# First product of the seven-product blocks in matmuls of 128 tokens instead of 256

## The chip, the cores and the metric

The kernel runs on one NeuronCore of a Trainium2 chip. The metric is the device time of one execution in microseconds. The kernel before took 926.25 us (median of three runs, 922.67 to 926.61).

## The reference, cut to what matters

The program computes a windowed attention with some global tokens, and passes its output through a two-layer network with an ELU between the layers:

```python
x = np.ascontiguousarray(attn_out.transpose(0, 2, 1, 3)).reshape(B * S, H * D)   # 8 * 544 tokens, 512 wide
h = x @ w_in                                                                     # 512 -> 2048
g = np.where(h > 0.0, h, alpha * (np.exp(np.minimum(h, 0.0)) - 1.0))
return (g @ w_out).astype(np.float32)                                            # 2048 -> 512
```

The attention has 8 batches of 8 heads, 512 local tokens and 32 global tokens of width 64; a local token sees the local tokens within 32 places of it and the global ones.

## The kernel before, in words

**Precision.** The network's operands are split into two f16 parts, a high and a low one (xh and xl for the tokens, win[0] and win[1] for the first weights, and so on). A product is made of three f16 products: high by high, low by high, high by low. All add up in one f32 bank of PSUM. In the profile, winh and winl are the two parts of the first weights.

**Blocks.** The tokens are cut into 17 blocks of 256 (NBL = 16 and one of global tokens). For each block the function ffn1 makes the first product, for one pair p of 128-column groups of the 2048 hidden columns at a time (eight pairs, NP = 8). Its result h has hidden columns on the 128 partitions, and j (which group of the pair) and 256 tokens along a row of one PSUM bank. The weights are the stationary operand: each matmul loads 128x128 of them (LDWEIGHTS, in the profile on the engine named PEld) and streams the tokens. For each j, four row groups c of the 512 inputs times three part products make 12 matmuls, so a pair has 24 (line 316). ScalarE then makes relu, copy and exp of h (lines 326 to 328).

**Two kinds of second product.** Early blocks, while the weights are still being converted, use the plain second product (ffn2, line 440, 512 columns a matmul); their h lies in a tile named h. From about 291 us on, blocks use a product of 2 x 2 quarters with seven multiplications instead of eight (ffn2_seven, line 475, table SEVEN). For these the job carries a list `seven`, and h is taken from the pool ps_a, as a tile named pa. The quarters are sums and differences of 128-token halves of the two groups j, made by VectorE (lines 335 to 351), scaled to a high f16 part by ScalarE (line 354) and a low one by VectorE (line 338). A pair's second product has 21 matmuls of 256 columns. The last pair of the last block has a function of its own, ffn1_last (line 394).

**Order of the work.** ffn_stream is a generator. A pair of a block is one call of ffn1, then the ffn2_seven of an older pair; each yields several times, ffn1 in the middle of each j, between the two j and at the end. The main loop at the end of attn_ffn takes a step of the attention and then as many steps of ffn_stream as the table PACE (and a few holds and alignments, such as `at[0]`) ask for. So the attention's score matmuls (line 734), value matmuls (795) and transposes (789, 721) stand between pieces of the network's matmuls, in the order in which the generators yield. Much of the rest is put off by a number of steps with defer.

**PSUM flags.** A matmul with start set begins a sum; with start unset it adds to the columns, or, where these have not been written since the bank was begun, writes them.

Of the kernel before, what the change touches and what calls it, by code (L numbers as in the profile page):

```python
# [22 lines left out]
P = 128  # L23
# [4 lines left out]
BLK = 256  # L28
NC = DM // P
# [31 lines left out]
def attn_ffn(ctx: ExitStack, tc: tile.TileContext, qT, qgT, kT, vT, w_in, w_out, mask, out):  # L61
    nc = tc.nc
# [22 lines left out]
    def defer(n, fn):  # L85
        if n == 0:
            return fn()
        later.setdefault(now[0] + n, []).append(fn)
# [11 lines left out]
    at = [None]  # L100
# [15 lines left out]
    def turn(name, tiles):  # L116
        turns[name] += 1
        return tiles[turns[name] % len(tiles)]
# [23 lines left out]
    win = [wts.tile([P, NC, DF], F16, name=f"win{k}") for k in "hl"]  # L142
# [155 lines left out]
    def ffn_stream():  # L298
# [3 lines left out]
        def ffn1(job, p):  # L302
            group, blk, xh, xl, sc, seven = job
            if (blk, p) == (order[-1], NP - 1):
                yield from ffn1_last(job, p)
                return
            if seven is not None:
                h = ps_a.tile([P, 512], F32, name="pa").rearrange("p (j t) -> p j t", j=2)
            else:
                h = ps_h.tile([P, 2, BLK], F32, name="h")  # L310
            for j in range(2):
                f = slice((2 * p + j) * P, (2 * p + j + 1) * P)
                k = 0
                for c in range(NC):
                    for wt, xt in ((win[0], xh), (win[0], xl), (win[1], xh)):
                        nc.tensor.matmul(h[:, j, :], wt[:, c, f], xt[:, c, :], start=k == 0, stop=k == 11)  # L316
                        k += 1
                        if k == 6:
                            at[0] = None
                            yield  # L320
                if j == 0:
                    yield
            g = ffn.tile([P, 2 * BLK], F32, name="g", bufs=2)
            hs = turn("hs", hss)
            hf = h.rearrange("p j t -> p (j t)")
            nc.scalar.activation(g, hf, AF.Relu, scale=sc[:, p:p + 1])  # L326
            nc.scalar.activation(hs, hf, AF.Copy, scale=sc[:, 2 * NP + 1 + p:2 * NP + 2 + p])
            nc.scalar.activation(g, g, AF.Exp, scale=-1.0)  # L328
            sg = sc[:, NP + p:NP + p + 1]
            shape = [P, 2 * BLK] if seven is None else [P, 7, P]  # L330
            gh = ffn.tile(shape, F16, name="gh", bufs=3)
            gl = ffn.tile(shape, F16, name="gl", bufs=3)

            def elu(out, *ins):
                nc.vector.scalar_tensor_tensor(out=out, in0=ins[0], scalar=-1.0, in1=ins[1], op0=ALU.add, op1=ALU.max)  # L335

            def low(dst, src, hi):
                nc.vector.scalar_tensor_tensor(out=dst, in0=src, scalar=sg, in1=hi, op0=ALU.mult, op1=ALU.subtract)  # L338

            def plain():  # L340
                elu(g, g, hs)
                nc.scalar.activation(gh, g, AF.Copy, scale=sg)
                defer(1, lambda: low(gl, g, gh))

            def parts():

                gx, q = quarters()
                elu(q, *(a.rearrange("p (a x) -> p a x", x=P) for a in (g, hs)))
                nc.vector.tensor_add(gx[:, 2:4, :], q[:, 0:2], q[:, 2:4])  # L349
                nc.vector.tensor_sub(gx[:, 5:7, :], q[:, 0:4:2], q[:, 1:4:2])  # L350
                nc.vector.tensor_add(gx[:, 0, :], q[:, 1], q[:, 2])  # L351

                def high():
                    nc.scalar.activation(gh, gx, AF.Copy, scale=sg)  # L354

                def lows():
                    low(gl, gx, gh)
                    seven.append(p)

                defer(2, high)  # L360
                defer(4, lows)

            defer(*(2, plain) if seven is None else (4, parts))
            pend.append((job, p, gh, gl))
            yield

        def quarters():


            a = ffn.tile([P, 10, P], F32, name="gx", bufs=1)  # L370
            return a[:, 2:9, :], a[:, 0:10:3, :]
# [248 lines left out]
        while left <= NBL:  # L620
            load()
            job = job or choose()
            if job is None:
                yield True
                continue
            cur, job = job, None
            group, blk = cur[:2]
            lo, hi = GROUPS[group]
            for p in range(lo, hi):
                load()  # L630
                yield from ffn1(cur, p)
                if len(pend) > LAG2:
                    yield from ffn2()
                    if twice[0]:
                        twice[0] = False
                        if pend[0][1] in (pend[0][0][5] or ()):
                            yield from ffn2()
                if p == hi - 1:
                    job = choose()
            if group in "ef":  # L640
                del xs[blk]
                left += 1
# [324 lines left out]
    f = ffn_stream()  # L967
# [105 lines left out]
```

## Time and profile before

| | |
|---|---|
| median of three runs | 926.25 us |
| the profiled execution | 926.27 us |
| its span, first to last instruction | 924.5 us |
| TensorE (PE) busy | 95% of the span |
| weight loads (PEld) busy | 78% |
| VectorE (DVE) busy | 76% |
| ScalarE (ACT) busy | 69% |
| GpSimd (POOL) busy | 19% |
| mean granted TensorE clock | 0.984 |

A row of the groups has line, engine, operation, tile written and tiles read, size, number of instructions, then busy time and mean length of one, then idle time of the engine ahead of them and what ended it. PE is the matmul itself, PEld the load of its weights, which overlaps other matmuls. A matmul's record lasts longer than the time until the next one starts. The table of stretches has one row for a stretch of time, with each engine's busy time and number of instructions. A row of the chain of waits has start, length, and the engine, tile and line of a piece of the work that ended last. A row of the waits has who waited for whom, us in total, times, and the longest.

### The profile page before, as it was taken

Reading aid. Unit: us, or ns where it says so; the run is one execution under the profiler, and the core shown is the slowest. Engines: PE = TensorE matmul, PEld = TensorE weight load, DVE = VectorE, ACT = ScalarE, POOL = GpSimd, SP = SyncE. Lnnn points to the kernel's source line nnn. Section 1 sums busy time; section 2 is a strip of 40 time slices with the busy share of each in tenths; the row PEclk is TensorE's granted clock in tenths of the full one; section 3 lists DMA queues with packets and bytes.
Section 4 is the critical chain, followed back from the end, with each engine's and each line's share of the span. In section 5 each row is a group of like instructions: output and inputs, shape, how many; then the busy total and the mean of one; then the engine's idle time right before and its main releaser. Section 6 shows DMA issues by size and latency. Waiting matters only on the chain.

```text
span 924.5 us, 26174 instructions
## 1 busy us (share of the span) xinstructions
PE 881.6 (95%) x10737; PEld 722.0 (78%) x10737; DVE 703.0 (76%) x1949; ACT 637.4 (69%) x1458; POOL 175.8 (19%) x237
## 2 busy tenths in 40 slices
PE   6889988899999999999999999999999999999997
PEld 3557655566666888888888888888888888888886
DVE  4987998898679878686777768676878677766566
ACT  5779987876666667666757667676767676656564
POOL 3343542424121201101101011110110011200000
PEclk8899999999999999999999999999999999999999
DMA  7977965635443144013321234104301111000000
GB/s 260 351 261 250 315 203 179 198 148 186 159 160 130 42 165 151 5 68 120 134 71 49 69 127 151 49 26 170 135 20 69 47 48 47 1 24 24 1 24 23
DMA packets 41775, 107.78 MB, mean 117 GB/s; under 512 B 6200, under 2 KB 6840, under 8 KB 41656
## 3 DMA queue, kind: packets, MB, share of 16 engines
q1 hardware_dynamic: 41368, 105.86, 33.1%
q8 instruction: 84, 1.38, 0.6%
q14 instruction: 35, 0.29, 0.1%
q10 hardware_dynamic: 288, 0.26, 0.1%
HBM read 88.80 MB, written 17.30 MB: 115 GB/s over the span
## 4 chain that ended last, share of the span: by engine, by line
PE 44%; DVE 28%; ACT 20%; issue 4%; DMA 3%; POOL 1%; SPq 0%; DVEq 0%; ACTq 0%; POOLq 0%
PE pa L316 17%; PE acc L475 8%; PE h L475 6%; ACT p L752 5%; ACT gh L354 4%; DVE gl L338 4%; DVE gx L335 3%; PE h L316 3%; PE acc L440 3%; ACT g L326 2%; PE pa L795 2%; ACT g L328 2%; DVE gx L349 2%; DVE cu L191 2%; PE pa L789 1%
## 5 line engine op out<-in xcount | busy, mean ns | idle before, releaser
L316 PEld LDWEIGHTS <-winh 128*128 128x128 f16 x2160 | 209.5, 98 | 32.9 <-issue 2.9
L316 PE MATMUL pa<-xh,winh 128*128 128x256 f16 x824 | 224.8, 273 | 0.3 <-DVE xglob L865 0.2
L316 PE MATMUL pa<-xl,winh 128*128 128x256 f16 x824 | 224.6, 273 | 0.0
L316 PE MATMUL pa<-xh,winl 128*128 128x256 f16 x824 | 224.6, 273 | 0.0
L354 ACT ACTIVATE gh<-gx,xs 128x896 f16<-128x896 f32 x103 | 107.5, 1044 | 134.4 <-DVE gx L351 134.4
L338 DVE SCALAR_TENSOR_TENSOR gl<-gx,xs,gh 128x896 f16<-128x896 f32 x103 | 122.7, 1191 | 73.2 <-ACT gh L354 73.2
L475 PEld LDWEIGHTS <-gh 128*128 128x128 f16 x1456 | 140.2, 98 | 22.7 <-issue 7.2
L758 POOL TENSOR_TENSOR p<-p,sm 128x512 f32<-128x512 f32 x64 | 72.4, 1134 | 343.9 <-DVE sm L757 310.9
L752 ACT ACTIVATE p<-p,m 128x128 f32<-128x128 f32 x256 | 99.3, 390 | 27.9 <-DVE m L746 27.8
L316 PEld LDWEIGHTS <-winl 128*128 128x128 f16 x1080 | 106.0, 98 | 13.1 <-issue 0.4
L475 PE MATMUL acc<-wouth,gh 128*128 128x256 f16 x312 | 85.2, 273 | 0.1
L328 ACT ACTIVATE g<-g 128x512 f32<-128x512 f32 x135 | 85.1, 631 | 0.0
L475 PE MATMUL acc<-wouth,gl 128*128 128x256 f16 x312 | 85.1, 273 | 0.0
L475 PE MATMUL acc<-woutl,gh 128*128 128x256 f16 x312 | 85.0, 273 | 0.0
L475 PEld LDWEIGHTS <-gl 128*128 128x128 f16 x728 | 71.2, 98 | 9.4 <-DVE gl L338 1.2
L326 ACT ACTIVATE g<-pa,xs 128x512 f32<-128x512 f32 x103 | 70.3, 682 | 8.8 <-PE pa L316 8.0
L475 PE MATMUL h<-raw,gh 128*128 128x256 f16 x416 | 74.3, 273 | 0.0
L316 PE MATMUL h<-xh,winh 128*128 128x256 f16 x256 | 70.6, 276 | 0.0
L316 PE MATMUL h<-xh,winl 128*128 128x256 f16 x256 | 70.6, 276 | 0.0
L316 PE MATMUL h<-xl,winh 128*128 128x256 f16 x256 | 70.5, 275 | 0.0
L795 PEld LDWEIGHTS pa<-pt,v 128*64 128x64 f32 x1728 | 52.9, 138 | 7.9 <-issue 5.9
L335 DVE SCALAR_TENSOR_TENSOR gx<-g,p 128x512 f32<-128x512 f32 x52 | 35.9, 691 | 27.4 <-ACT g L328 26.1
(228 smaller groups left out, 1891.4 us busy)
## 6 DMA issues: line engine op xcount, KB each, us to landing
v<-vT SPq DMA_DIRECT2D x64, 512.0 KB, 4.7
k<-kT SPq DMA_DIRECT2D x32, 640.0 KB, 5.3
q<-qT SPq DMA_DIRECT2D x32, 256.0 KB, 5.6
raw<-w_in SPq DMA_DIRECT2D x8, 1024.0 KB, 5.5
raw<-w_out SPq DMA_DIRECT2D x8, 1024.0 KB, 5.9
od<-o SPq DMA_DIRECT2D x32, 256.0 KB, 2.2
o<-od SPq DMA_DIRECT2D x32, 256.0 KB, 3.4
out<-o SPq DMA_DIRECT2D x32, 256.0 KB, 2.1
```

Source lines behind the costliest of these rows:

```text
L191: nc.vector.scalar_tensor_tensor(out=ui, in0=high, scalar=-0x40000000, in1=ui, op0=ALU.bitwise_and, op1=ALU.bitwise_or)
L316: nc.tensor.matmul(h[:, j, :], wt[:, c, f], xt[:, c, :], start=k == 0, stop=k == 11)
L326: nc.scalar.activation(g, hf, AF.Relu, scale=sc[:, p:p + 1])
L328: nc.scalar.activation(g, g, AF.Exp, scale=-1.0)
L335: nc.vector.scalar_tensor_tensor(out=out, in0=ins[0], scalar=-1.0, in1=ins[1], op0=ALU.add, op1=ALU.max)
L338: nc.vector.scalar_tensor_tensor(out=dst, in0=src, scalar=sg, in1=hi, op0=ALU.mult, op1=ALU.subtract)
L354: nc.scalar.activation(gh, gx, AF.Copy, scale=sg)
L440: nc.tensor.matmul(acc[t], gt[:, s], wt[:, f, :], start=p == first and j == 0 and k == 0, stop=p == last and j == 1 and k == 2)
L475: nc.tensor.matmul(cols, gt, w, start=p == 0 and k == 0, stop=last and k == len(todo) - 1, skip_group_check=True)
L752: nc.scalar.activation(ps[i], ps[i], AF.Exp, bias=m[:, i:i + 1], scale=-1.0, accum_out=s[:, 0, i:i + 1])
L758: nc.gpsimd.tensor_tensor(out=pp, in0=pp, in1=s[:, 1, :].unsqueeze(2).to_broadcast([P, 4, P]), op=ALU.mult)
L795: nc.tensor.matmul(o[:, to:to + n], st["v", g, t][:, 4 * h + w, :], st["pt", g, t][:, h, at:at + n], start=start, stop=True, skip_group_ch ...
```

## The change

In a block with `seven`, each matmul of the first product is cut into two of 128 tokens. In odd pairs the two halves of each step follow one another on the same weights; in even pairs all 12 matmuls of the first 128 tokens come first and then the 12 of the second. The other blocks and ffn1_last keep their 256 tokens. The yield inside a j comes after half of its matmuls, which is now the 12th of 24. The flag start is now set on the first matmul of the pair alone, since all four 128-column pieces share one bank.

```diff
             for j in range(2):
                 f = slice((2 * p + j) * P, (2 * p + j + 1) * P)
-                k = 0
-                for c in range(NC):
-                    for wt, xt in ((win[0], xh), (win[0], xl), (win[1], xh)):
-                        nc.tensor.matmul(h[:, j, :], wt[:, c, f], xt[:, c, :], start=k == 0, stop=k == 11)
-                        k += 1
-                        if k == 6:
-                            at[0] = None
-                            yield
+                todo = [(c, wt, xt, slice(0, BLK)) for c in range(NC)
+                        for wt, xt in ((win[0], xh), (win[0], xl), (win[1], xh))]
+                if seven is not None:
+                    halves = [slice(a * P, (a + 1) * P) for a in range(2)]
+                    todo = ([(c, wt, xt, a) for c, wt, xt, _ in todo for a in halves] if p % 2 else
+                            [(c, wt, xt, a) for a in halves for c, wt, xt, _ in todo])
+                n = len(todo)
+                for k, (c, wt, xt, a) in enumerate(todo):
+                    nc.tensor.matmul(h[:, j, a], wt[:, c, f], xt[:, c, a], stop=k == n - 1,
+                                     start=k == 0 and (j == 0 or seven is None), skip_group_check=seven is not None)
+                    if k == n // 2 - 1:
+                        at[0] = None
+                        yield
                 if j == 0:
                     yield
```

## The prediction, made before the changed kernel was run

> **What bounds the kernel now.** I read the page first (busy shares), then the table of stretches, to find the stretch that the change touches and what limits it there, then the groups of the changed line, and last the chain of waits and the timeline for the pace of single matmuls.
>
> ```profile
> span 924.5 us, 26174 instructions
> PE 881.6 (95%) x10737; PEld 722.0 (78%) x10737; DVE 703.0 (76%) x1949; ACT 637.4 (69%) x1458; POOL 175.8 (19%) x237
> L316 PE MATMUL pa<-xh,winh 128*128 128x256 f16 x824 | 224.8, 273 | 0.3 <-DVE xglob L865 0.2
> L316 PE MATMUL pa<-xl,winh 128*128 128x256 f16 x824 | 224.6, 273 | 0.0
> L316 PE MATMUL pa<-xh,winl 128*128 128x256 f16 x824 | 224.6, 273 | 0.0
> L316 PEld LDWEIGHTS <-winh 128*128 128x128 f16 x2160 | 209.5, 98 | 32.9 <-issue 2.9
> L316 PEld LDWEIGHTS <-winl 128*128 128x128 f16 x1080 | 106.0, 98 | 13.1 <-issue 0.4
> L316 PE MATMUL pa<-xh,winl x824: 271/273/273, 291.5 to 905.9; 128*128 128x256 f16 x165
> core 0: us, PE busy (x) PEld busy (x) DVE busy (x) ACT busy (x) POOL busy (x), PEclk, DMA share, GB/s
> 291.00:906.00 615.00, 609.58 (x7562) 533.95 (x7561) 453.14 (x1244) 414.68 (x916) 69.24 (x96) 1.00 0.21 72
> ```
>
> The first product of seven-product blocks writes tile pa; line 316 into tile h is that of the early blocks, which the change leaves alone. So the edit acts on 3 x 824 matmuls, from 291.5 to 905.9 us. A pair of weight columns takes 2 (j) x 4 (c) = 8 of each of the three forms, so 824 / 8 = 103 pairs. Thirteen blocks of eight pairs would be 104; the last one has its own function and isn't touched. Of the 103, 51 are odd (back to back) and 52 even (half by half).
>
> In that stretch the matmul engine is busy 609.58 of 615.00 us at a granted clock of 1.00: 5.42 us idle in all. Vector and scalar engine are at 74% and 67% there. So TensorE sets the time, and what matters is how many nanoseconds a matmul holds it, which is not the 273 ns of the groups: those records overlap. The pace is read from starts.
>
> ```profile
> 254.90 2.59 PE acc L440 x12
> ...
> 844.64 2.62 PE pa L316 x24
> 847.26 1.31 PE acc L475 x12
> 848.57 0.98 PE h L475 x9
> ...
> 893.76 2.62 PE pa L316 x24
> ```
>
> These are pieces of the chain of waits (start, length, what). From 844.64 to 893.76 lie ten rounds of 24 + 12 + 9 = 45 matmuls with 256 columns: 49.12 us / 450 = 109.16 ns each, with no gap: a stretch of nothing but back-to-back matmuls. The first row has matmuls of 512 columns: 2.59 / 12 = 215.8 ns.
>
> **The change part by part.**
>
> *Columns.* Every pair still streams 24 x 256 = 48 x 128 columns. Between 256 and 512 columns the pace rises by 215.8 - 109.16 = 106.7 ns for 256 columns, 0.4167 ns a column. Of the 109.16 ns, 106.7 are columns and 2.5 belong to the matmul itself. So 128 columns should take 53.3 + 2.5 = 55.8 ns: the columns cost what they did, and the 24 more matmuls of a pair pay 2.5 ns each. A pair goes from 24 x 109.16 = 2620 to 48 x 55.83 = 2680 ns, **+60 ns**. 103 pairs: **+6.2 us**. The rounding of 2.59 (0.005 in 12) moves the 2.5 by 0.4 ns, so this term lies between 5.2 and 7.2 us.
>
> *Weight loads.* The builder issues one load for each matmul, and consecutive matmuls on the same weights are not merged: before, wt = win[0] serves two matmuls in a row, and winh still has 2160 loads to winl's 1080. So 2472 loads come with the 2472 matmuls, also in the odd pairs. A load's record lasts 98 ns, and now has 55.8 ns of matmul to hide in. No row of the trace shows a load beside a 128-column f16 matmul, so its cost is bounded from both sides.
>
> ```profile
> 422.13 0.11 PEld L316 LDWEIGHTS <-winh 128*128 128x128 f16 x2
> 422.14 0.28 PE L316 MATMUL pa<-xh,winh 128*128 128x256 f16 x1
> 422.26 0.27 PE L316 MATMUL pa<-xl,winh 128*128 128x256 f16 x1
> 422.37 0.27 PE L316 MATMUL pa<-xh,winl 128*128 128x256 f16 x1
> 412.08 1.16 PE L734 MATMUL pa<-k,q 64*32 64x128 f32 x64
> 507.00 0.60 PE L789 MATMUL pa<-ident,p 128*128 128x128 f32 x4
> ```
>
> The low end is nothing. At 422.13, behind the attention's matmuls, nothing was loaded ahead: the load starts at 422.13, its matmul at 422.14, and the second load is over at 0.11 us, though each lasts 0.10. So the second load began some 0.01 us after the first: a load keeps the loader busy for about 10 ns, and the rest of its 98 ns is passage time that overlaps the next. The wholly unhidden first load costs 422.26 - 422.14 = 0.12 instead of 0.11 us. A gain is excluded: no column and no load goes away. The high end is the transposes: 128 columns and a load of 128 each, four with starts (0.60 - 0.27) / 3 = 0.11 us apart, as if the columns had not been halved. But they are 32-bit, and the kernel's line 316 is f16. I take nothing, by the rows at 422, which are the same weights on the same line; the high end stays as a rival.
>
> *Issue.* The 64 score matmuls at 412.08 start within 1.16 - 0.27 = 0.89 us, 14 ns for a load and a matmul. The sequencer can feed a pair every 55.8 ns four times over. Cost: nothing; without that cover it would be a pace, as in the rival on loads.
>
> *Instruction fetch.*
>
> ```profile
> q8 instruction: 84, 1.38, 0.6%
> q14 instruction: 35, 0.29, 0.1%
> ```
>
> 1.67 MB for 26174 instructions is 64 bytes each; 4944 more are 0.3 MB, a fifth of queues that use under 1% of the DMA engines. Nothing, hidden under the matmuls queued ahead.
>
> *Waits and order.* The half-way hand-over to the attention comes after 12 of 24 matmuls instead of 6 of 12, at the same time within the pair. No wait, DMA or queue is moved; the first matmul of a pair waits for its pa bank as before, and scalar line 326 for the last. One start flag for the bank instead of two is no instruction. What the longer pairs do to TensorE's own waits is a small gain:
>
> ```profile
> PE pa L789 <- DVE xg L865: 1.4, 1, 1.4
> PE pa L686 <- DVE xg L865: 1.4, 2, 1.1
> PE pa L789 <- DVE xglob L865: 1.4, 3, 0.7
> PE pa L789 <- issue: 0.6, 1, 0.6
> PE pa L316 <- DVE xglob L865: 0.2, 1, 0.2
> ```
>
> These are all of TensorE's waits between 291 and 906: eight, 5.0 us. They are for VectorE and would shrink by what the pairs just ahead of them grow. At most one grown pair (60 ns) each: 0 to 0.5 us; I take 0.3.
>
> *Sum.* +6.2 - 0.3 = +5.9 us on the profiled execution's 926.27 us (span 924.5 and 1.8 around it; the median of the three runs is 926.25, so no correction): **932.2 us**, 0.64% more.
>
> **The rivals.**
>
> *Loads that do not hide (slower by far).* If each load, or the pace of load and matmul together, shows at 128 columns, the price runs from the 10 ns at 422 (48 x 65.8 - 2620 = 538 ns a pair, 55 us, 982 us) over a pace of one load record, 98 ns (2084 ns a pair, 215 us, 1141 us), to the transposes' 109 ns (269 us, 1195 us). It decides if a load needs more than 55.8 ns from the start of the matmul before it. For it: the 98 ns record is longer than 55.8, and the only 128-column rows with full loads are at 109. Against it: two loads in 0.11 us, and at 256 columns not even a nanosecond of load shows in 109.16. Chance 0.08. The Trainium skill ("TensorE: Matmul & The Clock Gate", Back-to-back issue gap) states such a pace: streams of load and matmul sustain about 81 ns at 128 columns and about 131 ns at 512. By it a pair would take 48 x 81 = 3888 ns, 131 us more in all, some 1057 us. This trace contradicts the 512 figure with 215.8 ns, and agrees with the same section's isolated gap, columns over 2.4 GHz plus about 2.5 ns; no run here shows the 128 yet.
>
> *The same bank columns too soon (slower).* Half by half, each matmul adds to the 128 columns that the one before it just wrote, 55.8 ns later; before, and in the odd pairs, 109 to 112 ns pass. If that revisit needed the 109 ns, the 52 even pairs would take 48 x 109 = 5232 ns, +136 us, about 1062 us. No row shows such a limit. Chance 0.02.
>
> *TensorE's waits take up the growth (not slower).* If those eight waits end at times that the pairs' length does not move, the grown pairs fill them: 6.2 - 5.4 us of idle leaves 0.8, about 927.1 us. For it: the releaser is another engine. Against it: the reductions at line 865 follow TensorE's own value matmuls, so they move with it, and it takes 6.2 / 8 = 0.8 us, 13 grown pairs between cause and wait, at each. It decides from about three grown pairs ahead of each wait on (1.3 us in eight), where the growth falls under half a percent. Chance 0.05.
>
> **How the numbers follow.** The forecast has 0.85. Its own spread: 1 us from the rounding above, 0.2 from the waits, and the three runs before lie 3.9 us apart (922.67 to 926.61), so some 2 us each way, and as much for small shifts of the other engines' order: about 928.5 to 936. The range goes down to 927 for the third rival and stops at 938; the two dear rivals (0.10) stay outside. I call half a percent, 4.6 us, the bound of what a measurement of this kernel can tell from no change. The forecast's +5.9 is only 1.3 us above it; with a spread of about 2 to 2.5 us three quarters of its chance lie beyond: 0.63, and with the dear rivals 0.73. Within the bound 0.20 of the forecast and the third rival's 0.04: 0.24. Faster: 0.03, from the scatter alone.
>
> **What would show it.** Line 316 into pa should have three forms of 128x128 at 1648 each, winh 3808 and winl 1904 loads in all, records of about 273 - 53 = 220 ns, and 24-matmul stretches of the chain replaced by 48 in 2.68 us in odd and even pairs alike. A round of pair and second product in the last stretch should take 4.97 instead of 4.91 us. The granted clock stays 1.00. A pair over 2.8 us, or odd and even pairs that differ, makes the step on loads or on columns wrong; a span that grows by less than 4 us with pairs at 2.68 us makes the step on waits wrong; a pair under 2.62 us makes the whole reading wrong.

## The result, and the profile after

The changed kernel takes 931.91 us (median of seven runs, 930.47 to 935.56) against 925.69 us before (seven runs, 921.99 to 926.61). The medians differ by 6.2 us, the means of the seven runs by 7.3 us. The ratio is 1.0079, as of the means, with a 95% interval of 1.0057 to 1.0102: 5 to 9 us slower. The forecast was 932.2 us, in a range of 927 to 938.

In the changed kernel the matmul of line 316 is line 321, and all lines behind it have moved down by five too. The page of the changed kernel, with the rows that answer to those of before:

```profile
span 929.5 us, 31119 instructions
PE 885.5 (95%) x13209; PEld 754.9 (81%) x13209; DVE 704.1 (76%) x1949; ACT 638.1 (69%) x1458; POOL 174.9 (19%) x237
q8 instruction: 104, 1.70, 0.7%
L321 PEld LDWEIGHTS <-winh 128*128 128x128 f16 x3808 | 289.4, 98 | 17.6 <-issue 3.3
L321 PE MATMUL pa<-xh,winh 128*128 128x128 f16 x1648 | 254.9, 219 | 1.1 <-DVE xg L870 1.1
L321 PE MATMUL pa<-xl,winh 128*128 128x128 f16 x1648 | 255.3, 219 | 0.0
L321 PEld LDWEIGHTS <-winl 128*128 128x128 f16 x1904 | 169.2, 98 | 3.6 <-issue 0.5
```

The counts are those forecast: 1648 matmuls of 128 columns of each form, 3808 and 1904 loads, 2472 more of each kind in all. A matmul's record is shorter by 54 ns (219 instead of 273). Busy time alone says little: TensorE's share is 95% as before. Next the row of the table of stretches for the seven-product part of the changed kernel, and pieces of its chain of waits near the end:

```profile
291.00:911.00 620.00, 614.05 (x10003) 567.69 (x9996) 451.47 (x1240) 414.11 (x914) 68.78 (x96) 1.00 0.21 72
```

```profile
848.91 2.68 PE pa L321 x48
851.59 1.31 PE acc L480 x12
852.90 0.98 PE h L480 x9
853.88 2.68 PE pa L321 x48
...
898.63 2.68 PE pa L321 x48
```

Ten rounds from 848.91 to 898.63 take 49.72 us, 4.972 us each, where ten rounds took 49.12 us before. That is 60 ns a pair. Less 21 x 109.16 ns for the second product, 48 matmuls take 2680 ns, 55.8 ns each. Even and odd pairs alternate in these rounds, and every one of the ten has 2.68. Over all 103 pairs of the trace the median, from start to start, is 2680 ns for even and for odd pairs (2620 ns for both before).

To see where the rest of the difference lies, I cut the execution at the first and the last start of a first-product matmul into pa (the stretch), and summed from each matmul's start to the next start, by kind of matmul. The kernels before and after were each profiled a second time, unaltered; both executions of each are shown (us, worked out from the traces' start times):

```
                    before   2nd      changed  2nd
stretch begins at   291.26   290.02   289.02   293.87
stretch lasts       614.68   614.77   622.01   622.09
  first product     271.93   271.93   278.10   278.10
  second product    235.08   235.03   235.82   235.87
  transposes of p    17.64    17.63    18.33    18.35
  all others         90.14    90.29    89.81    89.82
behind the stretch   18.56    18.54    18.48    18.48
```

(A wait counts to the matmul before it. The four sums exceed the stretch by 0.05 to 0.11 us, since they take in the step behind its last matmul.) Two things are to be seen. The stretch repeats to a tenth of a microsecond: it grows by 7.3 us, of which 6.2 are the first product's pace. And what scatters from one execution to the next lies ahead of it: in these four executions of two kernels that are alike there, its begin lies anywhere between 289.02 and 293.87 us. The two profiled spans, 929.5 and 924.5 us, therefore differ by 7.3 in the stretch, less 2.2 of an earlier begin and 0.1 behind it.

TensorE's waits in the stretch of the changed kernel (us in total, times, longest):

```profile
PE pa L794 <- DVE xglob L870: 1.5, 2, 1.3
PE pa L794 <- DVE xg L870: 1.3, 1, 1.3
PE pa L691 <- DVE xg L870: 1.1, 1, 1.1
PE pa L321 <- DVE xg L870: 1.1, 2, 0.5
PE pa L794 <- issue: 0.5, 1, 0.5
PE pa L726 <- DVE xglob L870: 0.3, 1, 0.3
```

They sum to 5.8 us, where they were 5.0 before. A new one is the third from the end: the first product itself now waits twice for VectorE's line 870 (865 before), the reduction that frees a pa bank, 1.1 us in all, where before it waited once, 0.2 us.

### The profile page after: what moved, and what is told of

The parts are those of the page before. It is cut to its first block, busy times and chain, and to the rows that moved or that the text cites. A ratio compares the mean times of both kernels' runs of the same rounds, so it can differ in the third digit from the quotient of the medians.

```text
span 929.5 us, 31119 instructions
## 1 busy us (share of the span) xinstructions
PE 885.5 (95%) x13209; PEld 754.9 (81%) x13209; DVE 704.1 (76%) x1949; ACT 638.1 (69%) x1458; POOL 174.9 (19%) x237
## 4 chain that ended last, share of the span: by engine, by line
PE 61%; DVE 21%; ACT 12%; issue 3%; DMA 2%; POOL 1%; SPq 0%; DVEq 0%; ACTq 0%; POOLq 0%
PE pa L321 25%; PE acc L480 12%; PE h L480 9%; PE pa L800 4%; ACT p L757 3%; PE acc L445 3%; PE h L321 3%; DVE gl L343 2%; PE pa L794 2%; PE pa L739 2%; ACT gh L359 2%; DVE cu L191 2%; DVE gx L340 1%; DVE cu L195 1%; ACT g L331 1%
## 5 line engine op out<-in xcount | busy, mean ns | idle before, releaser
L321 PEld LDWEIGHTS <-winh 128*128 128x128 f16 x3808 | 289.4, 98 | 17.6 <-issue 3.3
L321 PE MATMUL pa<-xh,winh 128*128 128x128 f16 x1648 | 254.9, 219 | 1.1 <-DVE xg L870 1.1
L321 PE MATMUL pa<-xl,winh 128*128 128x128 f16 x1648 | 255.3, 219 | 0.0
L321 PE MATMUL pa<-xh,winl 128*128 128x128 f16 x1648 | 254.8, 219 | 0.0
L321 PEld LDWEIGHTS <-winl 128*128 128x128 f16 x1904 | 169.2, 98 | 3.6 <-issue 0.5
L480 PEld LDWEIGHTS <-gh 128*128 128x128 f16 x1456 | 137.0, 98 | 21.0 <-issue 6.8
```

The lines of the kernel that those rows point to most:

```text
L321: nc.tensor.matmul(h[:, j, a], wt[:, c, f], xt[:, c, a], stop=k == n - 1, start=k == 0 and (j == 0 or seven is None), skip_group_check=sev ...
L480: nc.tensor.matmul(cols, gt, w, start=p == 0 and k == 0, stop=last and k == len(todo) - 1, skip_group_check=True)
```

## The experiments

My theory was the forecast's: a matmul holds TensorE for its columns plus 2.5 ns, its load hides, and TensorE sets the time. The rivals were a price for the loads, and waits or order as the cause.

**The cut drawn further: 64 and 32 tokens.** The one line, here for 64:

```diff
-                    halves = [slice(a * P, (a + 1) * P) for a in range(2)]
+                    halves = [slice(a * 64, (a + 1) * 64) for a in range(4)]
```

> The first product of the seven-product blocks in matmuls of 64 tokens (96 a pair instead of 24), odd pairs on the same weights back to back, even pairs quarter by quarter. Theory (a matmul holds TensorE for its columns at 0.4167 ns each plus 2.5 ns, the load is hidden, TensorE sets the time): 26.7 + 2.5 = 29.2 ns each, a pair 96 x 29.2 = 2800 ns against 2620 before, +18.6 us over 103 pairs, about 944 us. Rival (a load keeps the loader busy for 10 to 15 ns and shows as soon as a matmul has fewer than about 100 columns): 40 to 45 ns each, a pair 3840 to 4320 ns, 1051 to 1101 us. Rival (the +6 us of the change came from waits and order, not from the matmuls' own pace): no more than a few us over the changed kernel, 932 to 936 us.

> The same with 32 tokens a matmul (192 a pair). Theory, drawn out to 32 columns: 13.3 + 2.5 = 15.8 ns each, a pair 3040 ns, +43 us, about 969 us; the score matmuls with their loads started 14 ns apart, so the sequencer could just do it. Rival (a pair of load and matmul has a floor of its own): any pace above 15.8 ns; at 20 ns a pair takes 3840 ns and the kernel 1051 us, at 30 ns 5760 ns and 1249 us. The Trainium skill, TensorE: Matmul & The Clock Gate, section Wait - 56ns, not 53.3ns?, gives a floor of about 25 ns from start to start however few the columns: by it a pair takes 4800 ns and the kernel about 1150 us.

With 64 tokens the kernel took 951.62 us (ratio 1.0278, 1.0242 to 1.0314), with 32 tokens 1163.04 us (1.2571, 1.2520 to 1.2623). The chain of waits of the first, then of the second:

```profile
907.61 2.80 PE pa L321 x96
```

```profile
1124.18 4.79 PE pa L321 x192
```

2.80 / 96 is 29.2 ns, the theory's pace to the digit; a load still costs nothing beyond the theory's 2.5 ns, beside 29 ns of matmul. 4.79 / 192 is 24.9 ns, not 15.8: at 32 tokens, load and matmul together don't get down to the theory's pace. The 25 ns of the Trainium skill ("TensorE: Matmul & The Clock Gate", Wait — 56ns, not 53.3ns?) agree with it. The time at 64 tokens came out 7 us over the theory's 944, and 952 lies outside both rivals too. Its stretch takes 642.35 us, 27.7 more than before: 18.6 are pace, 2.6 more lie in the first product, and 6.5 net in other kinds, with 5.5 more behind transposes of p. TensorE's waits in it are 8.1 us for VectorE and 4.2 us for nothing that the profile shows, where the kernel before has 4.4 and 0.6; why they grew was not tried. TensorE's waits in the stretch with 32 tokens, first row:

```profile
PE pa L321 <- issue: 11.0, 12, 2.0
```

These, too, are waits for nothing that the profile shows, in the middle of the first product; with two smaller rows they make 12.5 us. The pace alone, 4.79 instead of 2.62 us in 103 pairs, would add 223 us; the median is some 237 us above that of before, and the waits are about the difference. I come back to them below.

**The second product cut instead, in the kernel before.**

```diff
+                todo = [(gt, w[:, a * P:(a + 1) * P], n, a) for gt, w, n in todo for a in range(2)]
-                for k, (gt, w, n) in enumerate(todo):
-                    cols = acc[i][:, n * 256:(n + 1) * 256]
+                for k, (gt, w, n, a) in enumerate(todo):
+                    cols = acc[i][:, n * 256 + a * P:n * 256 + (a + 1) * P]
```

> The kernel before, with the second product of the seven-product blocks (not the first) cut from 256 to 128 columns a matmul: 42 matmuls a pair instead of 21, 104 pairs, other weights (gh and gl) and other banks. Theory: 104 x 21 x 2.5 ns = +5.5 us, 931 us. Rival (what the change cost lies in the first product's order, flags or bank): no difference, 925.7 us.

929.56 us, ratio 1.0041 (1.0026 to 1.0056), which is 2.4 to 5.2 us: slower, as the theory has it and the rival not, but less than 5.5. Its chain of waits:

```profile
893.67 1.34 PE acc L476 x24
895.01 1.00 PE h L476 x18
```

42 matmuls in 2.34 us are 55.7 ns each, the 55.8 of the theory within the rounding. The stretch grows from 614.7 to 618.4 us, and the second product's sum by 3.3 us, where its pace alone adds 2100 x 2.5 = 5.2: some 2 us of its waits went away. So the pace carries over to other weights and banks, and the waits can move either way.

**One more load for each matmul.** First placed freely, then kept in its place in TensorE's queue:

```diff
+                    if seven is not None:
+                        nc.tensor.ldweights(wt[:, c, f])
+                        tc.keep_in_program_order(nc.tensor.ldweights(wt[:, c, f]))
                     nc.tensor.matmul(h[:, j, a], wt[:, c, f], xt[:, c, a], stop=k == n - 1,
```

(The first run has the first of the two load lines, the second run the second.)

> The changed kernel with one more weight load ahead of each of the cut matmuls (the same weights loaded twice; the result of the first of the two isn't used): 4944 loads more. Theory (2.5 ns belong to the matmul, a load holds the loader for 10 to 15 ns and hides beside 55.8 ns): no difference to the changed kernel, 932 us. Rival (the 2.5 ns belong to the load): 4944 x 2.5 = +12 us, 944 us. Rival (a load isn't hidden once two must fit): 10 to 15 ns each, +49 to +74 us, 981 to 1006 us.

> The changed kernel with one more load of the same weights ahead of each cut matmul, now kept in its place (in loads2 the ones whose weights were ready early went to the front of TensorE's queue). Where two loads did stand ahead of one matmul in loads2, about 512 us, matmuls started 57.7 ns apart. Theory (a second load nearly hides): 4944 x 1.9 = +9 us on the changed kernel, 941 us. Rival (a load holds the loader so long that the pair falls to the pace of loads alone, 42 ns from load to load): 84 ns a matmul, +139 us, 1071 us. Rival (loads are free): 932 us.

The first, 1032.79 us (1.1141, 1.1108 to 1.1173), lies above all three forecasts and answers nothing about the price of a load. Its table of stretches shows why:

```profile
30.00:50.00 20.00, 0.32 (x4) 19.51 (x419) 1.90 (x2) 1.98 (x4) 1.26 (x1) 0.50 0.29 112
83.90:112.60 28.70, 0.46 (x5) 28.69 (x627) 2.63 (x7) 1.54 (x7) 1.87 (x2) 0.56 0.23 85
```

Loads that wait for no data but the weights were put in bunches of hundreds early in the queue, 46 to 48 ns a load, with hardly a matmul among them and the granted clock at 0.50 and 0.56 (0.99 and 1.00 at the same times in the changed kernel). The second, 944.63 us (1.0190, 1.0135 to 1.0246), does. Its chain of waits and its loads:

```profile
852.80 2.77 PE pa L323 x48
```

```profile
852.64 0.10 PEld L322 LDWEIGHTS <-winh 128*128 128x128 f16 x1
852.69 0.10 PEld L323 LDWEIGHTS <-winh 128*128 128x128 f16 x1
852.70 0.10 PEld L322 LDWEIGHTS <-winl 128*128 128x128 f16 x1
852.74 0.10 PEld L323 LDWEIGHTS <-winl 128*128 128x128 f16 x1
```

48 matmuls take 2.77 us, 57.7 ns each: a second load costs 1.9 ns beside 128 columns, 9.4 us in the first product's sum (287.48 against 278.10). That is the theory's price, and neither the free load of the one rival nor the other's 42 ns a load. The interval, 12 to 23 us over the kernel before, is wide; the pace and the sum decide. The 1.9 ns were read beforehand from the first run, so it is their repeating over all the matmuls that is new. Whether the 2.5 ns of every matmul are its own or those of its one load stays open: no run has a matmul without a load. But the two loads for one matmul start 43 ns apart, while the next matmul's load follows 15 ns behind (the commonest steps in the trace): it looks as if a load were quickly out of the way only when a matmul takes up its weights in between.

**Early blocks cut too.** The condition on `seven` dropped in the changed kernel, in the order of the matmuls and in their flags:

```diff
-                if seven is not None:
+                if True:
                     halves = [slice(a * P, (a + 1) * P) for a in range(2)]
...
-                                     start=k == 0 and (j == 0 or seven is None), skip_group_check=seven is not None)
+                                     start=k == 0 and j == 0, skip_group_check=True)
```

> The changed kernel with the first product of the early blocks cut to 128 tokens as well: 768 more matmuls and loads between 70 and 286 us, where TensorE idles 14 of 220 us. Theory: their pace is 55.8 ns too, +1.9 us of TensorE work, and 0 to 1.9 us of it shows, since part of that stretch waits for the weights' conversion: 932 to 934 us. Rival (where TensorE is not the bound, the finer matmuls help the mixing): 930 us or less.

937.48 us (1.0108, 1.0056 to 1.0160): inconclusive. The median is 5.3 us above that of the changed kernel in the same round (932.21, below), where the forecast allowed 2. But the interval holds the changed kernel's 1.0079 and the forecast 2 us above it, and the part that the edit touches is the part whose end moves by 5 us from one execution to the next: in this profile it ends at 293.45 us, between the two of the changed kernel. The stretch behind it, which the edit leaves alone, takes 623.67 us, 1.6 more than theirs; why was not tried. The rival's 930 us is out.

**Both kernels again.**

> The changed kernel once more, unaltered, for a second profile. Theory: the term of the first product in the seven-product stretch (from the start of each of its matmuls to the next start, summed) repeats to 0.1 us at 278.1, and what the second product and the transposes hold beyond their pace (0.7 us each over the kernel before in the first profile) moves by about a microsecond from one execution to the next. Rival: these two repeat as well, so the longer pairs make them. Time 932 us.

> The kernel before once more, unaltered, as a control. Time within 0.3% of the kernel before, 926 us; the first product's term 271.9 us; the start of the seven-product stretch (291.26 us in the first profile) and TensorE's waits in it differ by one or two microseconds.

932.21 us (1.0060, 1.0036 to 1.0085) and 924.79 us (0.9993, 0.9969 to 1.0017). The traces are the second and fourth column of the table above. The expectation on the waits was wrong: the sums of the second product and the transposes do not move by a microsecond between executions, they repeat to 0.05 us, so the 1.1 us beyond the pace belong to the changed kernel. That called for a theory of them.

**VectorE's order.** TensorE's queue holds the same kinds in the same order in both kernels through the stretch. VectorE's does not, in nine or so places. Here it is near 364 us, first in the kernel before:

```profile
363.66 0.34 DVE L865 TENSOR_REDUCE xg<-pa 128x32 f32<-128x64 f32 x2
363.92 0.67 DVE L867 TENSOR_REDUCE xm<-xr 128x1 f32<-128x512 f32 x1
364.84 1.15 DVE L338 SCALAR_TENSOR_TENSOR gl<-gx,xs,gh 128x896 f16<-128x896 f32 x1 [0.25 <-ACT gh L354]
```

and in the changed kernel, with TensorE's wait behind it:

```profile
363.41 0.22 DVE L870 TENSOR_REDUCE xg<-pa 128x32 f32<-128x64 f32 x1
364.60 1.15 DVE L343 SCALAR_TENSOR_TENSOR gl<-gx,xs,gh 128x896 f16<-128x896 f32 x1 [0.97 <-ACT gh L359]
365.67 0.22 DVE L870 TENSOR_REDUCE xg<-pa 128x32 f32<-128x64 f32 x1
```

```profile
365.94 0.27 PE L321 MATMUL pa<-xh,winh 128*128 128x128 f16 x2 [0.54 <-DVE xg L870]
```

The builder sets each engine's order, and with other matmuls it came out otherwise: the low part of a pair now stands between the two reductions. It waits 0.97 us for ScalarE, works 1.15 us, and the second bank comes free 2.3 us later than the first. Where TensorE starts the next first product, 0.81 us pass from start to start instead of 0.11; the same happens at 467 us. I moved the reductions up in the changed kernel and, as a control, in the kernel before:

```diff
-            defer(1, out)
+            def early():
+                with tc.high_priority(offset=BEHIND):
+                    out()
+
+            defer(1, early)
```

> The changed kernel with VectorE's reductions of the value product (they free its two pa banks) placed 60 instructions earlier in the builder's priorities; TensorE's queue stays as it is. In the changed kernel TensorE waits 0.81 us each near 365 and 467 us, where the second of two reductions stands behind the low part of a pair (1.15 us) in VectorE's queue; in the kernel before both reductions come first there. Theory (the waits beyond the matmuls' pace come from VectorE's order): the two reductions come first again, both waits fall to about 0.1 us, and the seven-product stretch (first to last start of its first product) shrinks from 622.0 to about 620.8 us; its first-product term stays 278.1. Rival (the longer pairs make the waits, whatever the order): 622.0 us again. The time, 932 us, moves less than its scatter.

> The same edit to the kernel before. Where its order already has both reductions first (near 364 and 465 us) nothing changes; elsewhere waits of 0.2 to 0.9 us in its 614.7 us stretch may go or come. Theory: 614 to 615 us, time 925 to 926 us. Rival (the order costs the kernel before as much as the changed one): 613.5 us or less.

Near 364 us the changed kernel's VectorE now has:

```profile
363.04 0.21 DVE L870 TENSOR_REDUCE xg<-pa 128x32 f32<-128x64 f32 x1
363.18 0.28 DVE L356 TENSOR_TENSOR gx<-gx 128x128 f32<-128x128 f32 x1
363.37 0.21 DVE L870 TENSOR_REDUCE xg<-pa 128x32 f32<-128x64 f32 x1
```

Both waits of 0.81 us are gone, and TensorE's waits for VectorE's line 870 no longer have a row of the first product:

```profile
PE pa L794 <- DVE xglob L870: 1.6, 2, 1.3
PE pa L794 <- DVE xg L870: 1.3, 1, 1.3
PE pa L691 <- DVE xg L870: 0.4, 1, 0.4
PE pa L726 <- DVE xglob L870: 0.3, 1, 0.3
```

The stretch is 620.69 us, as forecast; that of the kernel before is 615.01 us. The two waits are 1.4 us of it. Smaller ones came and went beside them (near 291 us 0.63 from start to start instead of 1.30; near 293 us a new 0.54; near 477 us 0.69 instead of 0.27), and the first product's sum is 278.59, not the forecast's 278.1. With the same rule for the reductions in both, the cut costs 5.7 us, 0.5 less than its pace. The times, 931.76 us (1.0056, 1.0041 to 1.0071) and 927.36 us (1.0004, 0.9993 to 1.0015; 925 to 926 had been expected), can't tell 1.3 us from none. No version of these beats the kernel before.

## Why the prediction was right, and where it was not

*What bounds the kernel.* Right: in a stretch with TensorE at 99%, 60 ns a pair came through in full.

*Columns.* Right: 55.8 ns a matmul, 2.68 us a pair, +6.2 us in both executions. Two rows, 512 and 256 columns, gave a line that held down to 64 columns (29.2 ns). That the 2.5 ns belong to the matmul itself, and not to its load, is not shown: no run parts them.

*Weight loads.* Right in what it took, nothing beyond the 2.5 ns; the pace with 64 tokens shows it. Its reason was too simple: a load does not leave the loader after 10 ns whatever follows. The sentence rested on two loads with a matmul between them; two loads for one matmul start 43 ns apart.

*The sustained pace of 81 ns.* The sustained pace of 81 ns at 128 columns in the Trainium skill ("TensorE: Matmul & The Clock Gate", Back-to-back issue gap) does not hold here; 55.8 ns does, which is that section's isolated gap, also with a load for every matmul.

*Issue and instruction fetch.* Right for this change (one wait for issue, 0.5 us, where there was one of 0.6), not for shorter matmuls (12.5 us at 32 tokens).

*Waits and order.* This step failed: it took 0.3 us off, and 1.1 us came on. It reckoned with growth hiding in TensorE's waits, which it took to be all for VectorE (one of them, 0.6 us, was for issue), and some of that happened: the transposes' waits near 426 and 527 us shrank from 0.94 and 0.75 us from start to start to 0.52 and 0.25. But it said that no queue is moved, and only TensorE's was not. The two waits of 0.8 us at 365 and 467 us were shown to come from VectorE's order by taking them away. A third, near 323 us (1.5 us instead of 0.5), stayed in reduce_first_after. There VectorE's maxima for the scores come behind a low part that they preceded in the kernel before; that this makes the wait was not tried, so the cause is shown for the two and open for the third.

*The sum.* +5.9 us was forecast, and the stretch grew by 7.3. That the median still fell within 0.3 us of the forecast is in part luck: what lies ahead of the stretch moves the time by up to 5 us from one execution to the next, more than the step on waits was off.

*The rivals.* Loads that do not hide, and bank columns too soon, would have made pairs of over 3 us, or even pairs unlike odd ones; neither is there (2680 ns for both). The waits did not take up the growth.

## What to carry to other kernels

Where TensorE is the bound, the price of cutting matmuls was here the number of added ones times a fixed gap (2.5 ns), and two widths in the trace were enough to read it off; the columns cost the same however they are cut. That held down to 64 columns, and not at 32. An edit to one engine's instructions can change another engine's order, so compare all engines' queues before calling a wait scatter. And profile the same kernel twice: what repeats to a tenth of a microsecond is likely to belong to the kernel, and a stretch that repeats shows differences that the total time can't.

## What the runs showed of the hardware that was not expected

At 32 columns, load and matmul together took 24.9 ns instead of the line's 15.8; at 64 the line still held. No narrower width was run, so that 25 ns is a floor for all of them is not shown here. At 25 to 29 ns a matmul TensorE also stops now and then (the longest wait is 2.0 us), for nothing that the profile shows. The packets of the instruction queue q8 (84 before, 104 after, 220 with 32 tokens) suggest what for. For the six longest such gaps with 32 tokens, from the trace (start of the gap and start to start, us; then how long before its end the last q8 packet started):

```
350.52  1.21   2.28
377.93  1.57   2.31
488.16  1.58   2.38
627.92  2.14   2.42
765.26  1.53   2.41
804.80  1.65   2.37
```

Each ends 2.3 to 2.4 us behind a packet of instructions, with packets 4.4 us apart in the stretch on the average (seven shorter gaps end 2.3 to 3.1 us behind one): it looks as if TensorE had run out of instructions and waited for that packet. No run took this apart, so it stays a reading.

Two loads ahead of one matmul started 43 ns apart at a granted clock of 1.00, and a second load cost its matmul 1.9 ns. Bunches of hundreds of loads with hardly a matmul ran at 45 to 48 ns each, at a granted clock of 0.50 to 0.58.
